# Gated recurrence on one core: score and value products cut into quarter-array products, units two deep

## The chip, the cores and the metric

The kernel runs on one core of a Trainium2 chip. The metric is the device time of one execution in microseconds. Engines are named as in the profile: PE (matrix products), DVE, ACT and POOL (vector, scalar and general engines), SP (the queue that issues most transfers). PE's weight loads are shown as PEld.

## The reference

Two blocks follow each other. The first is a gated linear recurrence over 4 batches, 8 heads, 768 tokens and head size 48; the second sends each of the 3072 tokens to the best of 8 experts.

```python
f = 1.0 / (1.0 + np.exp(-f_logit))
for t in range(S):
    state = f[:, :, t, :, None] * state + np.einsum('bhd,bhe->bhde', k[:, :, t], v[:, :, t])
    y[:, :, t] = np.einsum('bhd,bhde->bhe', q[:, :, t], state)
...
x = y.transpose(0, 2, 1, 3).reshape(3072, 384)
logits = x @ w_gate                       # 8 experts
expert_idx = np.argmax(logits, axis=1)
gate_w = softmax(logits)[arange, expert_idx]
h = np.maximum(x_sorted[lo:hi] @ w1[e], 0.0)      # 384 -> 1024, per expert
y_sorted[lo:hi] = h @ w2[e]                       # 1024 -> 384
out = gate_w[:, None] * y
```

## The kernel before, in words

The recurrence is done in 12 units. A unit is 128 tokens of two batches (16 heads, laid out as 8 slots with two heads of 64 partitions each, of which 48 are used). Units of even and odd number belong to the two pairs of batches, so a unit's state follows from the state two units earlier. All data are fp32, and every product on PE stands in the profile as two passes (a transposition as one).

For unit u these helpers exist; the lines are those of the profile:

- `load` (L410): f, k, q and v of the unit, on SP's queue. f has 2 buffers, k 3, q 4, v 3.
- `steps` (L420, L423, ACT): exp and ln of the gates. `total` (L430, DVE): their running sum, a scan of 1032 elements. `growth` (L444) and `decay` (L456), both ACT: exp of plus and minus that sum.
- `by_r` (L448, POOL): k times growth. `by_decay` (L468, DVE): q times decay. `ends` and `last_decay` (L451, L463): small copies on POOL.
- `score` (L473 to L483): k against q for half of the heads, eight products of 64 rows x 128 keys x 128 queries into two PSUM banks, and then DVE's `copy_predicated` under a causal mask into `at` (four such copies per unit, 512 elements each).
- `keys` and `keep` (L492 PE, L497 ACT): k transposed and copied to `kn`.
- `within` (L505): `at` with v into `yt`, 128 rows x 48 columns x 128 queries. `before` (L526): the old state with q, added to `yt`, 48 rows x 48 columns. `yt` is one buffer of two banks.
- `added` (L542) and `update` (L559 DVE, L561 POOL): the new state. `settle` (L567, ACT): the two copies of `yt` to `ys`.
- `rows` (L588 PE, L596 DVE): `ys` turned into rows of tokens (banks xp0 and xp1) together with the expert logits. `lay` (L613, L618, ACT) copies them to `xr`. Every second unit `choose` (L201 to L209, DVE), `weigh` (L241, ACT), `count` (L213, L214, PE into bank rp) and `settled` (`place` and `fill`, L220 to L247, DVE) find each token's expert and place, and `send` (L176) scatters the rows to `xs` on POOL's queue.

Three PSUM banks are handed round among kp0, kp1, xp0, xp1, dp and rp by `turns`; three more hold scores and two `yt`.

The order on every engine is written out by hand (`manual_schedule`): what a loop body calls first stands first on its engine. The loop of L687 runs n from 0 to 13, and its body works on unit n (scores, keys), unit n - 1 (`within`, `before`) and unit n - 2 (`settle`, `rows`, `lay`). On PE the order in the middle of the loop is: scores of the first half, kp, scores of the second half, xp, `within`, `before`, dp, and rp in every second step.

The last steps already start the experts: `soon` are the first rows of experts 0 and 1, loaded from `xs` when the scatters issued so far have landed; they are turned (etp), widened (L278) and narrowed (L292). After them 22 more expert tiles and two tiles of four parts each follow in an order of their own that the change does not touch. A fallback branch at the end is not taken.

Of the kernel before, what the change touches and what calls it, by code (L numbers as in the profile page):

```python
# [19 lines left out]
C = 128  # L20
NC = S // C
HP = H // 2
DP = 64

# [24 lines left out]
EARLY = 2  # L49
# [15 lines left out]
def _consts():  # L65
# [30 lines left out]
    m = {"causal": np.triu(np.ones((128, 128)))}  # L96
# [17 lines left out]
def kernel(  # L114
# [236 lines left out]
    with ExitStack() as st:  # L351
# [13 lines left out]
        scores = [wk.tile([128, 2, 2, HP, C], F32, name=f"at{i}", bufs=1) for i in range(2)]  # L365
        held = {
            n: [ld.tile([128, SEG, C], F32, name=f"{n}{i}") for i in range(bufs)]
            for n, bufs in (("q", 4), ("k", 3), ("f", 2))
# [10 lines left out]
        had, used = {"xp0": 0, "xp1": 1, "dp": 2, "rp": None}, [0, 1, 2]  # L379

        def turns(what, shape, steady=True):

            counts = had["rp"] is not None
            b = used[0]
            if steady:
                b = {
                    "kp0": had["dp"] if counts else had["xp0"],
                    "kp1": had["xp1"],
                    "xp0": had.get("kp0", 0),
                    "xp1": had["rp"] if counts else had.get("kp1", 1),  # L390
                    "dp": had.get("kp1", 1) if counts else had["dp"],
                    "rp": had["xp0"],
                }[what]
            had[what] = b
            if what == "dp":
                had["rp"] = None
            used.remove(b)
            used.append(b)
            return pst.tile(shape, F32, name=what, tag=f"tr{b}")

        def load(u, names, parts=(slice(None),)):
            x = units[u]
            for n in names:
                src = {"q": qu, "k": ku, "f": fu, "v": vu}[n]
                if n == "v":
                    x[n] = ld.tile([128, 2, H, D], F32, name=n, bufs=3)
                else:
                    x[n] = held[n][u % len(held[n])]
                for part in parts:
                    nc.sync.dma_start(x[n][:, part], src[u][:, part])  # L410
# [49 lines left out]
        def last_decay(u):  # L460
            x = units[u]
            x["last"] = wk.tile([128, SEG], F32, name="last", bufs=3)
            nc.gpsimd.tensor_copy(x["last"], x["dec"][:, :, C - 1])  # L463
# [9 lines left out]
        def score(u, a):  # L473
            x = units[u]
            x["at"] = scores[u % 2]
            ps = [pss.tile([128, HP, C], F32, name="s") for h in range(2)]
            for p, h, r in heads():
                s = HP * a + p
                nc.tensor.matmul(  # L479
                    ps[h][:, p], lhsT=x["k"][r, s], rhs=x["q"][r, s], start=True, stop=True  # L480
                )
            for h in range(2):
                nc.vector.copy_predicated(x["at"][:, a, h], _bc(causal, 1, HP), ps[h])  # L483

        def keys(u):
            x = units[u]
            x["kn"] = wk.tile([128, SEG, C], F32, name="kn", bufs=1)
            x["kp"] = []
            for a in range(2):
                kp = turns(f"kp{a}", [128, HP, C], u < NU - 2)  # L490
                for p in range(HP):
                    nc.tensor.transpose(kp[:, p], x["k"][:, HP * a + p], ident)  # L492
                x["kp"].append(kp)

        def keep(u):
            for a in range(2):
                nc.scalar.copy(units[u]["kn"][:, HP * a : HP * a + HP], units[u]["kp"][a])  # L497

        def within(u, a):

            x = units[u]
            if a == 0:
                x["yt"] = yt
            for p, h, _ in heads():
                nc.tensor.matmul(  # L505
                    x["yt"][DP * (h ^ a) : DP * (h ^ a) + D, a, p],
                    lhsT=x["v"][:, a, 2 * p + h],
                    rhs=x["at"][:, a, h, p],
                    start=p == 0,
                    stop=x["old"] is None,  # L510
# [3 lines left out]
        def before(u):  # L514

            x = units[u]
            if x["old"] is None:
                return


            for p in range(HP):
                for h in range(2):
                    for a in range(2):
                        r = slice(DP * h, DP * h + D)
                        to = DP * (h ^ a)
                        nc.tensor.matmul(  # L526
                            x["yt"][to : to + D, a, p],
                            lhsT=x["old"][r, HP * a + p],
                            rhs=x["q"][r, HP * a + p],
                            start=False,  # L530
                            stop=True,
                            skip_group_check=True,
                        )
# [17 lines left out]
        def update(u):  # L551

            x = units[u]
            new = wk.tile([128, SEG, D], F32, name="state", bufs=4)
# [8 lines left out]
        def settle(u):  # L563
            x = units[u]
            x["ys"] = wk.tile([128, 2, HP, C], F32, name="ys", bufs=1)
            for a in range(2):
                nc.scalar.copy(x["ys"][:, a], x["yt"][:, a])  # L567
# [3 lines left out]
        def rows(u):  # L571
# [12 lines left out]
            for a in range(2):  # L584
                j = 2 * (u - g[0]) + a
                xp = turns(f"xp{a}", [128, HP, XW], u < NU - 4)
# [9 lines left out]
                nc.vector.reduce_sum(  # L596
# [3 lines left out]
                )  # L600
# [27 lines left out]
        for i in (1, 0):  # L628
            nc.gpsimd.memset(scores[i], 0.0)
        warmth = pst.tile([128, C], F32, name="warmth", tag="tr2")  # L630

        def warm(count):

            for _ in range(count):
# [6 lines left out]
        load(2, "f")  # L641
        load(0, "v")
# [7 lines left out]
        for part in ab:  # L650
            steps(1, part)
        load(3, "f")
        load(2, "k")
        load(1, "v")
        load(2, "q")

# [10 lines left out]
        def settled(n, rt):  # L667
# [4 lines left out]
            if n == NU - 3:  # L672
# [7 lines left out]
            if n < NU:  # L680
# [5 lines left out]
        sends, later, decayed = [], None, None  # L686
        for n in range(NU + 2):  # L687
            here, back, last = n, n - 1, n - 2
            rt = None
            if here < NU:  # L690
                units[here]["old"] = states[here % 2]
            if 0 <= last:
                settle(last)
            if here < NU:
                score(here, 0)
            if 0 < n and n + 1 < NU:
                by_r(n + 1)
                ends(n + 1)
# [3 lines left out]
            if decayed:  # L702
                decayed()
                decayed = None
            if sends:
                now = sends if n >= NU - 1 else sends[:1]
# [3 lines left out]
            if n == 0:  # L710
                warm(2)
                keys(0)
                warm(4)
                for part in ab:
                    total(1, part)
                for part in ab:
                    growth(1, part)
                    by_r(1, part)
                    decay(1, part)
                    by_decay(1, part)  # L720
                    if part == ab[0]:
                        score(0, 1)
                warm(8)
                ends(1)
                last_decay(1)
                keep(0)
                steps(2)
                load(4, "f")
                load_consts()
                load_gate()  # L730
                load(3, "k")
                total(2)
                steps(3)
                growth(2)
            elif here < NU:
                if n == 1:
                    added(0)
                    decayed = update(0)
                keys(here)
                keep(here)  # L740
                score(here, 1)
            if 0 < n and n + 2 < NU:
                total(n + 2)
            if 0 <= last:
                rt = rows(last)
                if rt:
                    rt.choose()
            if 0 < n and n + 1 < NU:
                decay(n + 1)
                last_decay(n + 1)  # L750
            if 0 < n and n + 3 < NU:
                steps(n + 3)
            if 0 <= last:
                lay(last)
            if rt:
                rt.weigh()
            if 0 < n and n + 2 < NU:
                growth(n + 2)
            for a in range(2):
                if 0 <= back < NU:  # L760
                    within(back, a)
            if n == NU + 1:
                widen(soon[0], weights[0], early_h, range(3, 7))
            if n == NU:
                for x in soon:
                    turn_early(x)
            if 0 <= back < NU:
                before(back)
            if 0 < n and n + 1 < NU:
                for part in ab:  # L770
                    by_decay(n + 1, part)
            if n == 1:
                decayed()
            if 0 < here < NU and here // 2 < NC - 1:
                added(here)
                decayed = update(here)
            if rt:
                rt.count(turns("rp", [128, 2, rt.n, E], n < NU - 2))
                later = (n, rt)
                if n >= NU:  # L780
                    settled(*later)
                    later = None
# [381 lines left out]
```

## Time and profile before

| | us |
|---|---|
| median of 3 runs | 428.77 (427.64 to 429.92) |
| the profiled execution | 430.14 |
| its span, first to last instruction | 427.8 |
| PE busy in the span | 410.8 |
| DVE, ACT, POOL busy | 158.2, 105.3, 110.9 |
| n=2 and n=4 of the loop: first score starts | 28.23 and 47.46 |
| first product of the experts | 131.18 |
| first narrowing of an expert tile | 140.48 |

The profiled execution's time is 2.3 us above its span. In the tables of stretches each row is a stretch with its length, the busy time of PE, PEld, DVE, ACT and POOL with their instruction counts, the granted clock of PE (1.00 is full), the busy share of the DMA engines and their rate. In the timelines a row has start, length, engine, line, operation, written tile and read tiles, shape and count; a bracket tells how long the engine was idle before and what released it.

### The profile page before, as it was taken

What the parts mean: (1) busy time and instruction counts of PE and PEld (TensorE: products, weight loads), DVE (VectorE), ACT (ScalarE), POOL (GpSimd) and SP (SyncE); (2) the same over time, 40 slices, a digit from 0 to 9 for tenths busy, and PEclk for the clock granted to TensorE, in tenths of its full rate; (3) what the DMA queues carried; (4) which work ended last, traced back from release to release, by engine and by line L of the source; (5) the groups of instructions that cost most, each with busy time, mean ns of one, the idle gap of its engine ahead of it and who ended that gap; (6) DMA issues with size and microseconds to landing.
All of it is one profiled execution on the core that took longest, in us unless ns stands there. A gap on an engine that the chain in (4) does not pass through costs nothing.

```text
span 427.8 us, 8780 instructions
## 1 busy us (share of the span) xinstructions
PE 410.8 (96%) x3656; PEld 331.5 (78%) x3657; DVE 158.2 (37%) x365; ACT 105.3 (25%) x191; POOL 110.9 (26%) x121
## 2 busy tenths in 40 slices
PE   7979999999898999999999999999999999999992
PEld 7869888998788878888888888764888888888560
DVE  5887888888643521111111111211111111111110
ACT  6878766865332000000000000010000000000100
POOL 6484486779423200000000000000000000000000
PEclk9989999999998999999999999999999999999997
DMA  8969776869922369545695999810361399990000
GB/s 286 350 213 379 275 244 232 252 209 376 400 82 80 120 216 325 184 181 180 214 328 175 385 388 394 315 39 20 122 235 57 123 334 394 390 364 22 20 12 12
DMA packets 41982, 95.49 MB, mean 223 GB/s; under 512 B 3872, under 2 KB 27093, under 8 KB 41936
## 3 DMA queue, kind: packets, MB, share of 16 engines
q1 hardware_dynamic: 38448, 85.14, 56.2%
q0 software_dynamic: 3200, 9.64, 5.9%
q8 instruction: 30, 0.49, 0.5%
q10 hardware_dynamic: 288, 0.08, 0.1%
q14 instruction: 16, 0.13, 0.1%
HBM read 79.84 MB, written 15.40 MB: 223 GB/s over the span
## 4 chain that ended last, share of the span: by engine, by line
PE 91%; ACT 2%; DVE 2%; DMA 2%; POOL 1%; issue 1%; SPq 0%; POOLq 0%; ACTq 0%; DVEq 0%
PE hps L278 28%; PE yps L292 27%; PE xp L588 5%; PE s L479 5%; PE yt L505 5%; PE s L278 3%; PE yt L526 3%; PE kp L492 3%; PE yps L973 2%; PE hps L945 2%; PE yp L292 2%; PE etp L265 2%; PE dp L542 2%; DMA q<-in_qu_dram 2%; DVE sum L430 1%
## 5 line engine op out<-in xcount | busy, mean ns | idle before, releaser
L278 PEld LDWEIGHTS hps<-xT,w1t 128*128 128x128 f32 x1056 | 121.1, 192 | 7.3 <-issue 2.3
L278 PE MATMUL hps<-xT,w1t 128*128 128x128 f32 x1056 | 121.8, 275 | 0.0
L292 PE MATMUL yps<-w2t,hT 128*128 128x384 f32 x352 | 117.2, 486 | 0.0
L292 PEld LDWEIGHTS yps<-w2t,hT 128*128 128x128 f32 x352 | 65.2, 190 | 40.8
L176 POOL DMA_INDIRECT out_dram<-ysb,dst x26 | 25.3, 973 | 251.7 <-DVE ysb L299 251.7
L286 ACT ACTIVATE hT<-hps 128x512 f32<-128x512 f32 x22 | 13.2, 598 | 218.8 <-PE hps L278 218.8
L288 DVE TENSOR_SCALAR hT<-hps 128x512 f32<-128x512 f32 x22 | 15.2, 692 | 105.9 <-PE hps L278 105.9
L299 DVE TENSOR_SCALAR ysb<-yps,xrow 128x384 f32<-128x384 f32 x22 | 13.6, 618 | 92.9 <-PE yps L292 92.9
L176 POOL DMA_INDIRECT xs<-xr,posi x24 | 32.4, 1350 | 32.4 <-DVE lg L596 10.6
L483 DVE COPY_PREDICATED at<-mpack,s 128x512 f32<-128x512 uint8 x48 | 32.4, 728 | 14.3 <-PE s L479 10.9
L448 POOL TENSOR_TENSOR k<-k,r 128x1024 f32<-128x1024 f32 (+1 forms) x14 | 30.0, 2149 | 25.8 <-ACT r L444 25.7
L479 PE MATMUL s<-q,k 64*128 64x128 f32 x384 | 30.0, 290 | 5.3 <-DVE at L483 2.0
L479 PEld LDWEIGHTS s<-q,k 64*128 64x128 f32 x384 | 24.8, 191 | 9.0 <-DVE at L483 3.2
L430 DVE TENSOR_TENSOR_SCAN sum<-g,cap 128x1032 f32<-128x1032 f32 (+1 forms) x14 | 28.4, 2034 | 3.4 <-ACT g L423 3.4
L588 PE MATMUL xp<-fpack,ys 128*128 128x104 f32 x192 | 24.3, 280 | 0.8 <-ACT g L456 0.6
L588 PEld LDWEIGHTS xp<-fpack,ys 128*128 128x128 f32 x192 | 22.5, 192 | 2.2 <-issue 0.8
L505 PE MATMUL yt<-at,v 128*48 128x128 f32 x384 | 23.5, 275 | 0.0
L505 PEld LDWEIGHTS yt<-at,v 128*48 128x48 f32 x384 | 20.4, 123 | 1.2
L468 DVE TENSOR_TENSOR q<-q,g 128x512 f32<-128x512 f32 x24 | 17.6, 771 | 0.8 <-DMA q<-in_qu_dram 0.6
L267 DVE COPY xT<-etp 128x384 f32<-128x384 f32 x26 | 14.2, 548 | 3.2 <-remote 3.2
L567 ACT COPY ys<-yt 128x512 f32<-128x512 f32 x24 | 12.9, 593 | 9.7 <-PE yt L526 6.0
L497 ACT COPY kn<-kp 128x512 f32<-128x512 f32 x24 | 13.1, 602 | 5.5 <-PE kp L492 5.5
(113 smaller groups left out, 344.5 us busy)
## 6 DMA issues: line engine op xcount, KB each, us to landing
qw<-in_moe_w_dram SPq DMA_DIRECT2D x16, 1536.0 KB, 16.4
w1t<-in_moe_w_dram SPq DMA_DIRECT2D x8, 1536.0 KB, 6.8
w2t<-in_moe_w_dram SPq DMA_DIRECT2D x8, 1536.0 KB, 16.6
k<-in_ku_dram SPq DMA_DIRECT2D x12, 512.0 KB, 7.3
q<-in_qu_dram SPq DMA_DIRECT2D x12, 512.0 KB, 5.2
f<-in_fu_dram SPq DMA_DIRECT2D x11, 512.0 KB, 7.5
xrow<-xs SPq DMA_DIRECT2D x24, 200.0 KB, 7.5
xs<-pad SPq DMA_DIRECT2D x8, 600.0 KB, 3.5
```

What stands on the lines that cost most here:

```text
L176: ins = nc.gpsimd.indirect_dma_start(out=dst, out_offset=bass.IndirectOffsetOnAxis(ap=idx, axis=0), in_=src, in_offset=None, bounds_check= ...
L267: nc.vector.tensor_copy(x["xT"], tp)
L278: nc.tensor.matmul(hp[g][:, f, :], lhsT=w[0][:, j, b * 128 : b * 128 + 128], rhs=x["xT"][:, j, :], start=j == 0, stop=j == KD - 1,)
L288: nc.vector.tensor_scalar(x["hT"][:, 4:8], hp[1], 0.0, None, op0=OP.max)
L292: nc.tensor.matmul(yp, lhsT=x["hT"][:, f, :], rhs=w[1][:, f, :], start=f == 0, stop=f == NF - 1)
L430: nc.vector.tensor_tensor_scan(x["sum"][:, part].rearrange("p s c -> p (s c)"), x["g"][:, part].rearrange("p s c -> p (s c)"), cap[:, part ...
L448: nc.gpsimd.tensor_tensor(k, k, units[u]["r"][:, part], op=OP.mult)
L468: nc.vector.tensor_tensor(q, q, x["dec"][:, part], op=OP.mult)
L479: nc.tensor.matmul(ps[h][:, p], lhsT=x["k"][r, s], rhs=x["q"][r, s], start=True, stop=True)
L483: nc.vector.copy_predicated(x["at"][:, a, h], _bc(causal, 1, HP), ps[h])
L505: nc.tensor.matmul(x["yt"][DP * (h ^ a) : DP * (h ^ a) + D, a, p], lhsT=x["v"][:, a, 2 * p + h], rhs=x["at"][:, a, h, p], start=p == 0, st ...
L588: nc.tensor.matmul(xp[:, p], lhsT=x["ys"][:, a, p], rhs=wx[:, p, 0:XW] if a else wx[:, p, E:WX], start=True, stop=True,)
```

## The change

Scores and values are now products of a quarter of the array: 64 key rows by 64 (or 48) columns, on the four combinations of row group r and column group g. Keys are taken in halves. The first 64 keys meet all 128 queries ("long" products), the last 64 keys only the last 64 queries ("short" products); the masked quarter is not computed. So `at` has three parts in place of four, and three masks do the work of four. v gets a third copy in which halves are exchanged, so that keys and values stand on the same partitions.

`mix(n)` issues, in one run over the four quarters, the state products of unit n (`before`), the scores of unit n + 2 and the value products of unit n + 1 (`within`). Within that run `settle(n)` is called after the state products and the first mask after the scores of row group 0. A product of row group 0 into the third score bank is ordered behind the last mask (`behind`), because row group 1 writes the same bank earlier.

The banks are given out per step by `allot`. The loop has 10 steps; units 0 and 1 are started ahead of it, and the last two units are finished behind it by hand (`ordered_before`, `route`). k has 4 buffers, v 2, `state` 3, `last` 4. In the first loads v of unit 0, the constants and the gate weights now stand ahead of f of unit 2. In the profile of the new kernel the lines move: score L548 (long) and L558 (short), `within` L497 and L507, `before` L523, masks L606 and L611, dp L621, `update` L638, `settle` L646, xp L667 and L675, `lay` L693 and L698, kp L477 and L484, rp L215 and L216; the gates' lines L410 to L468 stay.

```diff
+    m = {"causal": np.arange(C)[None] >= p[:, None] % CH}
...
+        def allot(counts):
+            last = bank["dp"]
+            x, y = [b for b in used if b != last]
+            if counts:
+                bank.update(kp0=x, rp=y, kp1=last, xp0=x, xp1=last, dp=x)
+            else:
+                bank.update(kp0=x, kp1=y, xp0=last, xp1=x, dp=y)
...
-                    x[n] = ld.tile([128, 2, H, D], F32, name=n, bufs=3)
+                    x[n] = ld.tile([128, 3, H, D], F32, name=n, bufs=2)
...
+        def within(u, r, g):
+            x, on, i = units[u], slice(DP * r, DP * r + CH), g ^ r
...
+            def first(p):
+                nc.tensor.matmul(yt[DP * g : DP * g + D, r, p], lhsT=x["v"][on, 2 * r, 2 * p + i], rhs=x["at"][on, i, p], ...)
+            def second(p):
+                nc.tensor.matmul(yt[DP * g : DP * g + D, r, p, CH:C], lhsT=x["v"][on, 2 - r, 2 * p + i], rhs=late[on, HP * i + p], ...)
+            return [(2, first, p) for p in range(HP)] + [(1, second, p) for p in range(HP)]
...
+        def score(u, r, g):
...
+            def first(p):
+                nc.tensor.matmul(x["ps"][r][to, p], lhsT=x["k"][on, s, 0:CH], rhs=x["q"][on, s], ...)
+            def second(p):
+                ins = nc.tensor.matmul(late[to, HP * r + p], lhsT=x["k"][on, s, CH:C], rhs=x["q"][on, s, CH:C], ...).ins
+                if r == 0 and p == 0:
+                    behind(ins, x["masked"])
...
+        def mix(n):
+            score_banks(n + 2)
+            def parts(r, g):
+                long, short = score(n + 2, r, g)
+                inner = within(n + 1, r, g)
+                x = before(n, r, g)
+                if (r, g) == QUARTERS[-1]:
+                    x = x + [(0, settle, n)]
+                    inner = [(0, mask, n + 2, 0)] + inner
+                return x + short + long + inner if r else x + long + inner + short
+            run(parts)
...
         load(1, "kq")
+        load(0, "v")
+        load_consts()
+        load_gate()
...
-        load(2, "f")
-        load(0, "v")
+        load(2, "fk")
...
+        for n in range(NU - 2):
+            more = n < NU - 3
+            allot(bool(later))
+            by_decay(n + 3)
+            mix(n)
+            steps(n + 5)
+            mask(n + 2, 1)
+            mask(n + 2, 2)
+            load(n + 4, "q")
+            by_r(n + 3); ends(n + 3); last_decay(n + 3)
+            keys(n + 1, 0)
+            if later:
+                later[1].count(turns("rp", [128, 2, later[1].n, E]))
+            keys(n + 1, 1)
+            keep(n + 1)
+            if later:
+                settled(*later)
...
+            if sends: ...
+            total(n + 4)
+            rt = rows(n)
+            if rt:
+                rt.choose()
+                later = (n, rt)
+            lay(n)
+            if rt:
+                rt.weigh()
+            growth(n + 4); decay(n + 4)
+            added(n + 1)
+            update(n + 1)()
+            load(n + 5, "k"); load(n + 3, "v"); load(n + 7, "f")
+            if n in (5, 7):
+                load_weights((n - 5) // 2)
+        soon = [load_rows(slice(first[e], first[e] + C)) for e in range(EARLY)]
...
+        ordered_before(NU - 2, units[NU - 3]["summed"])
+        settle(NU - 2)
+        for x in soon:
+            turn_early(x)
+        later[1].count(...); settled(*later); ...
+        run(lambda r, g: within(NU - 1, r, g))
+        rt = route(NU - 2)
+        ordered_before(NU - 1, units[NU - 2]["summed"])
+        settle(NU - 1)
+        early_h = early_banks()
+        widen(soon[0], weights[0], early_h, range(3))
+        rt.count(...); settled(NU, rt)
+        rt = route(NU - 1)
+        widen(soon[0], weights[0], early_h, range(3, 7))
+        rt.count(...); settled(NU, rt)
+        widen(soon[0], weights[0], early_h, range(7, NF))
```

The loop's bounds on late units (`if n + 5 < NU` and the like) are left out here.

## The prediction

> **What bounds the kernel now.** I read the page's engine shares and slices first, then the busy time by stretch of two neighbouring steps, then the timeline of those steps on each engine.
>
> ```profile
> PE 410.8 (96%) x3656; PEld 331.5 (78%) x3657; DVE 158.2 (37%) x365; ACT 105.3 (25%) x191; POOL 110.9 (26%) x121
> PE   7979999999898999999999999999999999999992
> DVE  5887888888643521111111111211111111111110
> ...
> 66.30:75.45 9.15, 9.15 (x154) 8.21 (x153) 8.00 (x19) 5.73 (x12) 6.97 (x6) 1.00 0.70 259
> 75.45:85.15 9.70, 9.70 (x160) 8.72 (x157) 8.47 (x18) 8.33 (x16) 7.10 (x10) 1.00 0.80 243
> ```
>
> DVE's 37% is an average of two stages. In the recurrence (the first 13 slices, until the experts start near 131 us) it is 80 to 90% busy. In the two stretches (length, then busy us of PE, PEld, DVE, ACT and POOL, granted clock, DMA share) PE has no idle time and DVE only 1.2 us a step. After 140 us PE is full and the change does not reach it. So the forecast is the shift of that border.
>
> ```profile
> 75.45 1.16 PE L479 MATMUL s<-q,k 64*128 64x128 f32 x16
> 76.54 1.09 PE L492 MATMUL kp<-fpack,k 128*128 128x128 f32 x8
> 77.56 1.16 PE L479 MATMUL s<-q,k 64*128 64x128 f32 x16
> 78.65 2.03 PE L588 MATMUL xp<-fpack,ys 128*128 128x104 f32 x16
> 80.61 1.96 PE L505 MATMUL yt<-at,v 128*48 128x128 f32 x32
> 82.50 1.09 PE L526 MATMUL yt<-q,state 48*48 48x128 f32 x32
> 83.52 1.14 PE L542 MATMUL dp<-v,kn 128*64 128x48 f32 x32
> 84.59 0.41 PE L213 MATMUL rp<-oh,fpack 128*128 128x32 f32 x2
> ```
>
> Start to start this step is: scores 1.09 twice, kp 1.02, xp 1.96, yt 1.89 and 1.02, dp 1.07, and 0.56 for the rp pair in every second step.
>
> ```profile
> 68.75 0.74 DVE L220 COPY counts<-sums 128x8 f32<-128x8 f32 x1
> 70.88 0.18 DVE L247 RECIPROCAL xr<-su 128x4 f32<-128x4 f32 x1
> 72.19 2.30 DVE L430 TENSOR_TENSOR_SCAN sum<-g,cap 128x1032 f32<-128x1032 f32 x1
> 74.39 0.27 DVE L596 TENSOR_REDUCE lg<-xp 128x8 f32<-128x32 f32 x2
> 74.60 0.48 ACT L618 COPY xr<-xp 128x384 f32<-128x384 f32 x1 [2.35 <-DVE lg L596]
> 83.92 1.04 ACT L444 ACTIVATE r<-sum 128x1024 f32<-128x1024 f32 x1
> 84.86 1.06 ACT L567 COPY ys<-yt 128x512 f32<-128x512 f32 x2
> ```
>
> This is the chain to watch: L220 to L247 is `settled`, 2.31 us; the scan is 2.30; ACT's copy L618 starts 0.2 after the reduction; growth and the next copy stand 0.94 apart. Today xp ends at 71.5 and nobody on PE needs its banks for 3 us, because yt stands between xp and dp. The change moves yt away.
>
> **Products.** The records of L526 show four quarter products starting together every 109 ns, those of dp (64 columns of weights, 48 moving) two every 58 ns. A quarter now gets, per step, 12 long products (state, score, value) and 8 short ones (64 moving), each in two passes: 12 x 2 x 109 = 2.62 and 8 x 2 x 58 = 0.93, and 0.2 for the change of shape that every group shows: 3.75 us in place of 1.09 + 1.09 + 1.89 + 1.02 = 5.09. That is -1.34 a step. No row has short products on four quarters: if they go two at a time (29 ns each) the group is 4.7 us, if they run like the long ones in whole rounds 5.3, and 3.75 is the low end. I take 3.75, since four quarters at once are shown by L526 and 58 ns a round by dp; the rest goes into the range. The Trainium skill ("TensorEngine Tiling (Array Packing)", Instruction Overhead) speaks against short products: about 60 cycles each, 25 ns. By it the group is an estimated 4.2 us, and the sum some 5 us higher.
>
> DVE loses one mask of four, 0.68 us. v grows by half (192 KB a unit, 0.5 us at 370 GB/s); with 0.70 to 0.80 of DMA busy that stays hidden.
>
> **Where the gain goes.** The built program gives the waits. (a) The value products wait for both copies `settle`, which follow the state products of the same step. (b) In every second ("counting") step, the one with rp, dp shares its bank with xp0, so dp waits for ACT's L618 copy of xp0, which waits for DVE's reduction; on DVE, ahead of that reduction, stand the third mask, `settled` and the scan. (c) In the other ("choosing") step ACT's order is L618/L613, exp, growth, decay, and only then the next `settle`; exp waits for DVE's `choose` (1.2 us, six operations of 0.19). (d) The short scores of row group 0 wait for the first mask: it ends at 3.4 and 4.7 in the two steps below, PE arrives at 3.7 and 5.2, so this costs nothing until DVE is 0.3 later.
>
> Choosing step from its start 0: state products end at 1.07, settle 1.2 to 2.3, value products start at 2.4 (PE was ready at 1.96), the group ends 1.8 later at 4.2, kp and xp end at 7.15, dp at 8.2. DVE: third mask 4.3 to 5.0, scan to 7.3, reductions 7.6, choose 8.8. ACT: exp 9.0, growth and decay (0.96 each) 10.9.
>
> Counting step: ACT is free at 10.9 - 8.2 = 2.7, settle ends 3.75, value products start at 3.8: 1.85 us of PE lost. Group end 5.6, kp + rp + xp (3.54) 9.15. DVE: mask 5.7 to 6.35, settled to 8.7, scan 11.0, reduction 11.15, copy 11.65. dp starts 11.75, 2.6 us late, and ends at 12.8.
>
> Pair: 8.2 + 12.8 = 21.0 against 9.15 + 9.70 = 18.85. So PE's 2.7 us of a pair are returned, and 2.15 more. Behind dp on PE's queue stands the whole next group, so it is late next, and with it its masks; DVE itself would need only 16.4 (its operations of the pair with gaps 17.7, less two masks). POOL's product of k ends near 3.9 and is needed a step later. On SP the load of q goes at 1.1, lands after 5.2 to 7.5 and is needed 0.8 into the next step, so both are hidden, q with little to spare.
>
> **Sum.** Front: f of unit 2 is now issued behind v, the constants and the four gate loads, which wait for the constants. 4.3 MB lie ahead: 2.8 by 10 us, then 355 GB/s, so 14.4; gate loads 1.8 (their row), landing 3.5: 19.9 in place of some 17. k, v and f of unit 3 follow (1.6 MB, 24.4). ACT: steps of unit 3 to 26.6, growth and decay to 28.5; q times decay 1.3: the first new step starts at 30.1 (score of unit 2 now: 28.2). ACT then does unit 4's steps, growth and decay of unit 3 (after its scan, 32.2), settle to 35.3: the step ends at 41.3, the next at 50.3, where the old loop's n=4 starts at 47.46: +2.9. Three pairs: 63.0 for 56.6, +6.4. Step 8 (no scan, three small operations more): 11.0 for 8.7, +2.3. Tail, to the first `narrow_early` at 140.5: the old one takes 27.7 from 112.8 with broken PE work. Now step 9 takes 6.15; the last scatters leave POOL 14.1 after step 8's start, and as at present (113.46 to 119.2) rows can be fetched 5.7 later and land in 2.5; etp waits 4.3 us for that, then etp, rp, yt, xp, state, 8 blocks, xp and two rp: 19.9. 26.05 in all, -1.7. Together +9.9.
>
> **Clock.** PE's new idle times have a price of their own.
>
> ```profile
> 28.20:30.00 1.80, 1.77 (x19) 1.57 (x20) 1.51 (x3) 1.46 (x3) 1.80 (x2) 0.76 0.88 320
> 30.00:32.00 2.00, 2.00 (x13) 1.67 (x13) 0.84 (x2) 1.14 (x3) 2.00 (x3) 0.50 0.97 367
> ```
>
> The eighth column is the granted clock: 0.5 for 3.41 us, and kp there takes 1.97 for 1.02. It follows a 1.84 us gap; the 3.41 us stretch before it is 46% busy, another drop follows one of 61%, and stretches of 63 and 65% had none. Gaps of 1.85 and 2.6 us drop it about 0.8 and 1 times. A drop costs 1.7 us of work; I take half as hidden in the waits: 4 counting steps x 1.8 x 1.7 x 0.5 = 6.1, and 1.7 for the tail's gap: +7.8 (0 to 14). The Trainium skill ("TensorE: Matmul & The Clock Gate", HAM oscillation) has a half-rate clock only after gaps above about 3.4 us; by that alone nothing is lost in the steps, and the sum is +9.9 or a little more. The 1.84 us gap of this trace speaks against it.
>
> Total +17.7: the profiled execution takes 430.14 (span 427.8 and 2.3 around it) and would take 447.8; the median, 1.4 lower, becomes 446.5.
>
> **Rivals.**
> 1. Same stalls, clock stays up: +9.9, 438.7. For it: the drops need an unlucky place of the window. Chance 0.2.
> 2. Other side: the chain mask, settled, scan, reduction, copy does not reach dp. It decides once that chain takes under 3.6 us from the group's end in place of 6.1. Then DVE's 16.4 a pair bounds: 3 x -2.45, step 8 -1, tail -1.7, front +2.9: -7, 422. Against it: each member is a row above, and DVE runs in order. Chance 0.09.
> 3. Short products two at a time, or the half clock unhidden: 0.95 a step for ten steps, or 6 more: 453 to 456. Chance 0.13.
> 4. My case, 0.58.
>
> **Numbers.** 0.5%, 2.1 us, is about what a measurement can tell. Rival 2 holds 0.06 of faster and 0.03 of same; 0.02 of same comes from a cheaper front and tail: 0.06, 0.05, 0.89. The range runs from below rival 1 to rival 3's top: 435 to 457.
>
> **What would show it.** Right: dp (now L621) waiting over 2 us in every second step, released by L698; value products (L497) released by ACT's copy L646; choosing steps near 8 and counting steps near 13 us; 0.5 clock stretches between 50 and 130 us; etp late. Wrong: even steps of about 8.5 us, PE above 95% until 110 us, or the border before 131 us.

## The result, and the profile after

The changed kernel takes 455.62 us (454.23 to 456.75) where the kernel before takes 429.35: ratio 1.060, 95% interval 1.052 to 1.068. A second measurement gave 455.88 and 1.060 (1.052 to 1.068). The profiled execution took 456.75 with a span of 454.4; that is 26.6 longer than the span before.

The page's line of busy time and its rows of 40 slices (PE, DVE, granted clock):

```profile
PE 407.3 (90%) x4424; PEld 331.1 (73%) x4425; DVE 162.3 (36%) x343; ACT 104.1 (23%) x187; POOL 116.3 (26%) x121
PE   7767759695978799999999999999999999999992
DVE  6586776767573453111112111122111111221110
PEclk9968998989799989999999999999999999999998
```

PE is busy for 3.5 us less than before in a span that is 26.6 longer. The difference lies in the first 14 slices, before the experts: in most of them PE falls to 0.5 to 0.7, the clock dips in several, and DVE is busy for 4.1 us more in all, although it has one mask less in a unit. So PE waits, and the waits of PE say for what (line that waited, line that released it, us in total, times, longest):

```profile
PE yt L497 <- ACT ys L646: 13.0, 7, 3.9
PE s L558 <- DVE at L606: 9.6, 6, 5.0
PE dp L621 <- ACT xr L698: 7.0, 4, 2.2
PE xp L667 <- ACT ys L646: 2.3, 1, 2.3
```

The first is the wait for `settle`, (a) and (c) of the prediction, and the third is (b). The second, short scores behind the first mask, is (d), which I had at nothing. A counting step and the choosing step behind it, from PE's timeline:

```profile
60.99 0.27 PE L558 MATMUL s<-q,k 64*64 64x64 f32 x2 [0.76 <-DVE at L606]
61.60 0.66 PE L477 MATMUL kp<-fpack,k 128*128 128x128 f32 x4
62.94 2.03 PE L667 MATMUL xp<-fpack,ys 128*128 128x104 f32 x16
67.17 1.37 PE L621 MATMUL dp<-v,kn 128*64 128x48 f32 x32 [2.21 <-ACT xr L698]
68.48 1.96 PE L523 MATMUL yt<-q,state 48*48 48x128 f32 x32
```

xp ends at 65.0, dp starts at 67.17, and the state products behind it take 1.96 for 1.09: half clock. What stands behind the first of these waits is seen only when DVE and POOL are laid side by side:

```profile
57.72 2.59 DVE L468 TENSOR_TENSOR q<-q,g 128x1024 f32<-128x1024 f32 x1 [1.72 <-ACT g L456]
60.23 1.33 DVE L606 COPY_PREDICATED at<-mpack,s 128x512 f32<-128x512 uint8 x2
69.63 1.22 DVE L468 TENSOR_TENSOR q<-q,g 128x1024 f32<-128x1024 f32 x1
```

```profile
56.86 2.36 POOL L448 TENSOR_TENSOR k<-k,r 128x1024 f32<-128x1024 f32 x1
69.80 1.73 POOL L640 TENSOR_TENSOR state<-state,last 128x384 f32<-128x384 f32 x1 [0.73 <-DVE state L638]
```

DVE's product of q takes 1.22 us by itself. At 57.72 it meets POOL's product of k, which ends at 59.22, and it ends 1.1 us after that: it waited POOL out. Twelve us later DVE comes first, and POOL's small product takes 1.73 in place of 0.83. In the kernel before, the product of q stood at the end of a step, and POOL's product of k started after it had ended:

```profile
74.57 1.29 DVE L468 TENSOR_TENSOR q<-q,g 128x512 f32<-128x512 f32 x2
76.57 2.37 POOL L448 TENSOR_TENSOR k<-k,r 128x1024 f32<-128x1024 f32 x1 [0.44 <-ACT r L444]
```

In one table (us; a step starts with its state products, in the old loop with its first scores; steps 2, 4, 6, 8 of the new loop answer to n = 4, 6, 8, 10 of the old; "end" is the first `narrow_early`, the border behind which both kernels are alike):

| | step 2 starts | pair 2, 3 | pair 4, 5 | pair 6, 7 | step 8 | step 9 to end | end |
|---|---|---|---|---|---|---|---|
| before | 47.5 | 18.8 | 18.9 | 18.9 | 8.7 | 27.7 | 140.5 |
| predicted, clock left out | 50.3 | 21.0 | 21.0 | 21.0 | 11.0 | 26.05 | 150.4 |
| after | 54.95 | 23.4 | 22.3 | 25.3 | 12.3 | 28.2 | 166.35 |
| e1 dp's bank | 56.3 | 23.5 | 23.3 | 23.3 | 11.1 | 26.7 | 164.2 |
| e8 PE kept warm | 55.0 | 21.5 | 22.6 | 25.4 | 13.7 | 27.2 | 165.5 |
| e10 decay first | 53.8 | 21.4 | 22.0 | 23.9 | 12.9 | 26.3 | 160.4 |
| e9 all cures | 43.8 | 19.8 | 20.6 | 18.5 | 15.0 | 27.7 | 145.35 |
| e11 and late weights | 42.4 | 18.9 | 19.6 | 20.5 | 9.9 | 28.9 | 140.1 |

Steps 2 to 8 together take 65.3 us before, 74.0 as predicted without the clock, 83.2 after, 80.2 in e10, 73.8 in e9 and 68.8 in e11.

### The profile page after: what moved, and what is told of

It reads as the page before. It is cut to its first block, busy times and chain, and to the rows that moved or that the text cites. A ratio compares the mean times of both kernels' runs of the same rounds, so it can differ in the third digit from the quotient of the medians.

```text
span 454.4 us, 10248 instructions
## 1 busy us (share of the span) xinstructions
PE 407.3 (90%) x4424; PEld 331.1 (73%) x4425; DVE 162.3 (36%) x343; ACT 104.1 (23%) x187; POOL 116.3 (26%) x121
## 4 chain that ended last, share of the span: by engine, by line
PE 59%; DMA 1%; POOL 0%; DVE 0%; POOLq 0%; issue 0%
PE hps L280 26%; PE yps L294 25%; PE yps L1103 2%; PE hps L1075 2%; PE etp L267 2%; PE yp L294 1%; DMA out_dram<-ysb,dst 1%; DMA xrow<-xs 1%; PE hps L1094 0%; POOL out_dram L178 0%; DVE ysb L301 0%; POOLq L1142 0%
## 5 line engine op out<-in xcount | busy, mean ns | idle before, releaser
L290 DVE TENSOR_SCALAR hT<-hps 128x512 f32<-128x512 f32 x22 | 15.2, 692 | 106.2 <-PE hps L280 101.1
L178 POOL DMA_INDIRECT xs<-xr,posi x24 | 31.0, 1291 | 38.3 <-DVE xr L249 12.4
L468 DVE TENSOR_TENSOR q<-q,g 128x1024 f32<-128x1024 f32 (+1 forms) x14 | 29.1, 2087 | 13.7 <-ACT g L456 11.6
L448 POOL TENSOR_TENSOR k<-k,r 128x1024 f32<-128x1024 f32 (+1 forms) x14 | 29.7, 2126 | 16.6 <-ACT r L444 16.6
L497 PE MATMUL yt<-at,v 64*48 64x128 f32 x384 | 20.4, 292 | 13.3 <-ACT ys L646 13.0
L497 PEld LDWEIGHTS yt<-at,v 64*48 64x48 f32 x384 | 16.8, 132 | 14.9 <-ACT ys L646 14.7
L558 PE MATMUL s<-q,k 64*64 64x64 f32 x384 | 17.9, 239 | 10.2 <-DVE at L606 9.6
L667 PE MATMUL xp<-fpack,ys 128*128 128x104 f32 x192 | 25.0, 284 | 2.3 <-ACT ys L646 2.3
L548 PE MATMUL s<-q,k 64*64 64x128 f32 x384 | 24.8, 305 | 2.2 <-POOL rend L451 2.2
L667 PEld LDWEIGHTS xp<-fpack,ys 128*128 128x128 f32 x192 | 23.2, 196 | 3.1 <-ACT ys L646 2.4
L558 PEld LDWEIGHTS s<-q,k 64*64 64x64 f32 x384 | 15.9, 152 | 11.6 <-DVE at L606 10.7
L548 PEld LDWEIGHTS s<-q,k 64*64 64x64 f32 x384 | 20.3, 154 | 3.0 <-POOL rend L451 2.6
L621 PE MATMUL dp<-v,kn 128*64 128x48 f32 x320 | 12.6, 235 | 7.7 <-ACT xr L698 7.0
L621 PEld LDWEIGHTS dp<-v,kn 128*64 128x64 f32 x320 | 11.2, 148 | 9.1 <-ACT xr L698 7.6
```

Source lines behind the costliest of these rows:

```text
L178: ins = nc.gpsimd.indirect_dma_start(out=dst, out_offset=bass.IndirectOffsetOnAxis(ap=idx, axis=0), in_=src, in_offset=None, bounds_check= ...
L290: nc.vector.tensor_scalar(x["hT"][:, 4:8], hp[1], 0.0, None, op0=OP.max)
L448: nc.gpsimd.tensor_tensor(k, k, units[u]["r"][:, part], op=OP.mult)
L468: nc.vector.tensor_tensor(q, q, x["dec"][:, part], op=OP.mult)
L497: nc.tensor.matmul(yt[DP * g : DP * g + D, r, p], lhsT=x["v"][on, 2 * r, 2 * p + i], rhs=x["at"][on, i, p], start=p == 0, stop=False, skip ...
L548: nc.tensor.matmul(x["ps"][r][to, p], lhsT=x["k"][on, s, 0:CH], rhs=x["q"][on, s], start=True, stop=True,)
```

## Experiments

Theory A: the units two deep tie PE, ACT and DVE into a ring (decay, product of q, masks, `settled`, scan, reduction, ACT's copies, decay of the next step), and each named wait is only the place where PE feels it. Rivals: one wait alone is the price; or the half clock is; or the engines have no slack in any order. Four kernels ran on a chip where the kernel before takes 423.9 us, the others where it takes 428.6 to 430.2, so ratios are compared, and steps in the profile.

**after_again: the changed kernel once more.**

> The changed kernel itself, unedited, beside the three that follow, because the kernel before takes 429.4 us on one chip and 423.9 us on another. Expected: ratio 1.052 to 1.068 as at first, first narrow_early near 166 us in the profile.

455.88 us against 430.15; first `narrow_early` at 166.8. This is the yardstick.

**e1: dp in another bank.**

```diff
-                bank.update(kp0=x, rp=y, kp1=last, xp0=x, xp1=last, dp=x)
+                bank.update(kp0=x, rp=y, kp1=last, xp0=x, xp1=last, dp=y)
```

> In counting steps dp takes rp's bank instead of the bank of xp0. Theory A (DVE's chain mask, settled, scan, reduction sets the pace and the bank is only where PE feels it): the four dp waits for ACT's L698 (2.2, 2.2, 2.2, 0.35, together 7.0 us) go, but L698 stays as late as before, so exp, growth, decay and the settle of the choosing step behind it on ACT are as late, and the value products L497 of the choosing step, which waited 0 in step 3, wait some 2 us: 453 to 457 us. Theory B (the shared bank alone is the price): dp starts 2.2 us earlier, nothing takes the place of the wait, and two or three half-clock stretches of 3.41 us go with it: 444 to 449 us.

453.32 us, ratio 1.069 (1.067 to 1.071). The waits of PE from 20 to 140 us:

```profile
PE yt L497 <- ACT ys L646: 20.5, 10, 4.0
PE s L558 <- DVE at L606: 11.5, 9, 2.8
PE s L548 <- POOL rend L451: 0.4, 1, 0.4
```

```profile
PEclk9686999999899899999999999999999999999998
```

This is theory A: dp's 7.0 us are gone from the list, the value products wait 20.5 where the changed kernel's wait 12.7 in this stretch, and a pair is still 23.3 to 23.5. The granted clock is full here from 44 to 118 us, which speaks against the clock too.

**e2: `settled` and the sends behind `rows`.**

```diff
-            if later:
-                settled(*later)
...
             rt = rows(n)
+            if later:
+                settled(*later)
...
```

> settled and the sends are issued behind rows, so DVE reduces xp right after the scan and L698 copies xp0 some 2 us earlier; dp keeps its bank. Theory A (DVE's chain is the cause): dp's waits of 2.2 us fall below 0.5 us, ACT is early too, a counting step is 2.2 us shorter, three or four of them, and one or two half-clock stretches go: 444 to 450 us. Theory B (only the bank): the same for dp. Rival: settled now stands between the reductions and choose or the state update of dp, and the scatters leave later; the tail gives back 1 to 3 us: 450 to 455 us.

455.18 us, ratio 1.074 (1.068 to 1.081). dp waits 1.0 us in all for L698, but the short scores 13.9 and the value products 15.2. The expected 444 to 450 did not come: I had let DVE's 2.3 us of `settled` vanish, where by DVE's order they only move behind the reduction and ahead of the next product of q.

**e3 and e10: decay before growth.** The same kernel, on the chip of each group.

```diff
-                growth(n + 4)
                 decay(n + 4)
+                growth(n + 4)
```

(and alike for units 2 and 3 ahead of the loop, with `by_decay(2)` ahead of growth).

> ACT computes decay before growth, so DVE's product of q can start before POOL's product of k. Theory A (the product of q, 2.5 to 3.1 us beside POOL's product of k and 1.22 us alone, waits for POOL to finish, and this makes the first mask late): L468 falls to 1.2 to 1.5 us in the loop, the waits of the short scores L558 inside the loop (0.75 to 1.2 us in each step that has one) go, the first step starts some 1.3 us earlier: 447 to 452 us. Rival (the product of q is slow for another reason, such as the loads, or the first mask waits for the scores anyway): L468 stays at 2.5 us or more, or L558 waits as before: 454 to 457 us.

445.64 us, ratio 1.0527 (1.0485 to 1.0569).

> The exchange of growth and decay alone, once more, on the chip of these runs, because the kernel before took 423.9 us on the chip where it was run and 430 us where the changed kernel was. Theory A (DVE's product of q waits for POOL's product of k): 9 to 13 us under the changed kernel's 455.7, ratio 1.03 to 1.04 if the kernel before takes 430 us here. Rival (most of the 12 us seen in the profile were the chip's or the clock's luck): within 5 us of the changed kernel, ratio 1.048 or more.

452.44 us (449.84 to 456.74), ratio 1.0554 (1.0485 to 1.0623). DVE and POOL of this second run, at the same place as above:

```profile
55.66 1.23 DVE L468 TENSOR_TENSOR q<-q,g 128x1024 f32<-128x1024 f32 x1 [0.78 <-ACT g L456]
56.65 2.46 POOL L448 TENSOR_TENSOR k<-k,r 128x1024 f32<-128x1024 f32 x1 [0.85 <-ACT r L444]
```

The mechanism is shown: DVE comes first and needs 1.23, and POOL's product of k grows by 0.1 for an overlap of 0.24 us. In the three meetings shown in rows, and in two more of this run (77.32 and 78.31 us), the one that starts later grows by the overlap less 0.12 to 0.15. The mean of the ten whole products of q falls from 2.42 to 1.53. The waits of PE from 20 to 140 us, three of the lines:

```profile
PE yt L497 <- ACT ys L646: 12.8, 8, 4.0
PE dp L621 <- ACT xr L698: 7.0, 4, 2.3
PE s L558 <- DVE at L606: 5.9, 2, 4.6
```

Inside the loop one wait of the short scores is left, 1.3 us in step 7, where the product of q waited for the load of q and so came behind POOL again. The size is not what theory A asks for: 3.4 us by the median (5.3 if the longest of the four runs, 456.74, is left out), with intervals that overlap the changed kernel's, and 6 and 12 us at the border of the two profiles. The ratio of 1.055 is where the rival has it: most of the 12 us of e3's profile does not come back. dp still waits 7.0 and the value products 12.8 us: the rest of the ring stands.

**e4: growth and decay behind `settle`.**

```diff
             mix(n)
+            growth(n + 3); decay(n + 3)
...
             mask(n + 2, 2)
+            by_decay(n + 3)
...
-            growth(n + 4); decay(n + 4)
```

> growth and decay of unit n+3 are issued on ACT behind the settle of step n, and DVE's product of q behind the three masks. Theory A (the value products wait because settle stands behind growth and decay on ACT): the waits of L497 for L646 fall from 13.0 us in seven to under 4 us, first mask no longer late, L558 waits gone; dp still waits about 2 us in counting steps, where DVE's chain grows by the product of q: 440 to 450 us. Rival (DVE becomes the bound, as its product of q now waits for POOL's product of k at the place that the scan needs): steps of 11 us or more, 453 to 460 us.

446.37 us, ratio 1.055 (1.051 to 1.058), above the expected 440 to 450 once the faster chip is allowed for. L497's waits fall from 12.7 to 5.1 and the short scores' inside the loop to 0.3, but dp waits 8.3, and there is a new wait: xp for ACT's copies of kp (L484), 5.8 us, because growth and decay now stand ahead of them, besides `steps`.

**e5 and e8: products of a constant in PE's waits.** e5 puts 13 and 16 of them into each counting step, e8 6 and 8 (steps 0 and 1 have 24 and 13, and 15 and 6).

```diff
+        def busy(b, count):
+            warmth = pst.tile([128, C], F32, name="warmth", tag=f"tr{b}")
+            for _ in range(count):
+                nc.tensor.matmul(warmth, lhsT=pad[:, 0:C], rhs=pad[:, 0:C], start=True, stop=True)
...
+                    inner = [(0, busy, bank["kp0"], count)] + inner     # ahead of the value products
...
+                if counting:
+                    busy(bank["rp"], 8)
                 added(n + 1)
```

> Products of a constant are put on PE into its waits: 13 ahead of the value products of every counting step (24 and 13 in the first two steps) and 16 ahead of dp in counting steps, each some 0.11 us at full clock, so about as long as the waits of 1.75 and 2.2 us. Nothing else moves. Theory A (the clock that the waits cost has a price of its own, 6 us in the steps): half-clock stretches fall from eight windows of 3.41 us to five or fewer, waits for DVE and ACT keep their ends, and the time is 3 to 7 us under the changed kernel. Rival (the half clock falls into time that PE would wait anyway): fewer stretches, but within 1.5 us of the changed kernel, or later by the dummies that overrun a wait.

457.45 us, ratio 1.064 (1.057 to 1.072), no half clock from 30 us on. But one such product took 0.24 us, not 0.11, so they were 1.4 to 1.6 us longer than the waits of 1.75 and 2.2 us, and this run settles nothing.

> The products of a constant again, in a number that fits the waits: one took 0.24 us, so 6 (1.5 us) ahead of the value products of a counting step, 8 (1.9 us) ahead of its dp, 15 and 6 in the first two steps. Theory A (the half clock has a price of its own; the run with twice as many paid it back by overrunning each wait by 1.4 us): choosing steps at 8.1 us in place of 9.4 to 9.8, counting steps at 12 to 13, a pair 20.5 to 21.5 us in place of 23.4, first narrow_early at 158 to 163 us, 4 to 8 us under the changed kernel. Rival (the ring of waits sets the pair and the clock is hidden in it): a pair stays at 23 us, within 1.5 us of the changed kernel.

454.45 us, ratio 1.056 (1.054 to 1.059). Its waits from 20 to 140 us (lines stand 6 later here: L612, L627, L652 and L704 are L606, L621, L646 and L698) and its clock by slices:

```profile
PE s L558 <- DVE at L612: 9.2, 7, 3.8
PE yt L497 <- ACT ys L652: 2.5, 6, 1.0
PE dp L627 <- ACT xr L704: 1.2, 3, 0.4
```

```profile
PEclk9869999999999989999999999999999999999998
```

From 33 to 158 us there is no half clock, where the changed kernel has 17 us of it between 37 and 120. Choosing steps 3 and 5 take 8.2 and 8.3 in place of 9.8 and 9.4, the length predicted for full clock. But up to the start of step 8 the choosing steps gain 2.2 us in all and the counting steps lose 0.8, step 8 takes 1.4 more, and the border comes 0.9 us earlier; by the medians it is 1.4 us, with intervals that overlap. By the time the rival is right. The price of the clock itself is bounded, not measured: in step 6 these products end 1.2 us behind the `settle` that the value products wait for (in step 4 too, but there a wait for the first mask follows), in step 8 1.4 us behind the copy that dp waits for. With these added back, an estimate of 0.9 to 3.5 us is left. Most of the half clock in the loop lies in time that PE has to wait anyway.

**e6: ACT's order, dp's bank and both together.** Decay ahead of growth behind `settle`, `steps` behind `keep`, dp in bank y:

```diff
             mix(n)
+            decay(n + 3); growth(n + 3)
-            steps(n + 5)
...
             keep(n + 1)
+            steps(n + 5)
```

> All three waits of the loop at once: ACT's order is settle, decay and growth of unit n+3, the copies of kp, then the steps of unit n+5; DVE's product of q stands behind the masks; dp takes rp's bank in counting steps. Theory A (each single cure only moved the wait to the next member of a ring of ACT, DVE and PE; with all of them PE is the bound again): dp's and the short scores' waits gone, value products at most 0.7 us late, a pair of steps 18.5 to 20 us in place of 23.4, first narrow_early at 142 to 150 us: ratio 1.00 to 1.035. Rival (DVE's and ACT's own work, some 8.2 us a step plus the product of q waiting for POOL, bounds the loop now): a pair stays at 21 us or more and new waits for DVE or ACT appear: ratio 1.045 or more.

448.02 us, ratio 1.042 (1.035 to 1.049): between the two, in its pairs (20.1 to 23.1) as well. The value products still wait 15.9 us from 20 to 140. `settle` stands right behind ACT's copies of xp, these are behind DVE's reduction, and that is behind the product of q, which meets POOL's again (2.7 us), and the scan.

**e7: the same, and the constants behind unit 2's loads.**

```diff
         load(0, "v")
-        load_consts()
-        load_gate()
...
         load(2, "q")
+        load_consts()
+        load_gate()
```

> The same as the run before it, and the constants and gate loads are issued behind f, k and q of unit 2, so SP does not wait for the constants ahead of f of unit 2. Theory A (the front is set by f of unit 2, which is issued at 16.6 us): f of unit 2 is issued near 6 us, the first step starts 4 to 7 us earlier, and the whole shift reaches the end: 4 to 7 us under the run before it. Rival (what is loaded later, f of unit 3, q of unit 2 or the constants, becomes late instead, or the DMA engines are full until 13 us anyway): at most 2 us.

444.88 us, ratio 1.035 (1.027 to 1.044). f of unit 2 is issued at 6.1 us in place of 16.6, and step 2 starts 2.5 us earlier than in e6. f of unit 4 is now the one behind the gate loads: it is issued at 24.9 in place of 21.9. The gain of 3.1 us lies between the two expectations.

**e9: all cures.** To e7 are added: the gate loads behind v of unit 2, `settle(0)` ahead of the loop, decay first for unit 2, and in the loop

```diff
             mix(n)
+            if later:
+                later[1].weigh()
...
             mask(n + 2, 1)
+            by_decay(n + 3)
             mask(n + 2, 2)
-            by_decay(n + 3)
...
-            total(n + 4)
             rt = rows(n)
             if rt:
                 rt.choose()
+            total(n + 4)
             lay(n)
-            if rt:
-                rt.weigh()
```

> All cures together: ACT settle, decay, growth, copies of kp, steps; the first settle already in the prologue; dp in rp's bank; DVE takes the product of q between the second and third mask, before POOL's product of k can start, and the scan behind choose; the exp of choose goes behind the next settle; f of unit 2 ahead of the constants, and the gate loads behind f of unit 4. Theory A (the products themselves are 0.9 us a step cheaper and only the ring of waits and the front ate it): steps of 8.7 to 9.5 us, first step near 25 us, first narrow_early at 132 to 141 us, ratio 0.98 to 1.01. Rival (DVE, ACT and PE each have about 8.5 us of work a step, and any order leaves some wait): steps of 10 us or more, ratio 1.02 to 1.035.

433.70 us, ratio 1.007 (1.004 to 1.010). Its largest waits of PE from 20 to 140 us, six of its lines:

```profile
PE s L558 <- issue: 4.7, 4, 2.7
PE yt L497 <- ACT ys L646: 2.5, 8, 0.4
PE xp L667 <- ACT ys L646: 2.2, 1, 2.2
PE rp L215 <- issue: 1.9, 1, 1.9
PE yt L523 <- issue: 1.2, 2, 0.9
PE yt L497 <- issue: 0.9, 3, 0.4
```

22 of the 26 us are back. The three waits of the loop are down from 29.3 us (L497, L558 and L621 in the changed kernel, 20 to 140 us) to 3.5. Of the 21.0 us by which the border comes earlier, 11.1 lie ahead of step 2, where no run cured the loads alone, and 9.4 in steps 2 to 8. The ratio is where theory A has it, but the steps, 8.9 to 11.3 us and 15.0, are longer than its 8.7 to 9.5: the ring accounts for about half of the loss, and for the steps the rival is not refuted. Step 2 starts 3.6 us ahead of the kernel before; the steps behind it still take 8.5 us longer than that kernel's, 6.3 of this in step 8. What is left has no partner engine: PE stands for 9 us, 6.8 of it at its quarter products, and the rows name no cause.

**e11: weights of the second expert later.**

```diff
-            if n in (5, 7):
-                load_weights((n - 5) // 2)
+            if n == 5:
+                load_weights(0)
         soon = [load_rows(...) for e in range(EARLY)]
+        load_weights(1)
```

> The kernel with all cures, and the weights of the second expert are loaded behind the rows of the first tiles instead of in step 7, where DMA is full. In the run with all cures PE stands for 9 us in the loop and tail at its quarter products without a wait that the profile names (issue), the longest 2.68 us in step 8 while the DMA engines are full with these weights, followed by 3.4 us of half clock. Theory C (PE's own instructions are fetched over the full DMA engines): the 2.68 us and the half clock behind it go, issue waits fall to 5 to 6.5 us: 4 to 5 us less, 428 to 430.5 us, ratio 0.995 to 1.002. Rival (the stalls have another cause, such as a wait that the profile does not record): issue waits stay at 8 us or more and the time within 1.5 us of 433.7; or the later weights make the second expert wait: above 435.

431.23 us, ratio 1.0046 (1.0007 to 1.0085), against e9's 1.0073 (1.0044 to 1.0102). Step 8 falls from 15.0 to 9.9 and the stall of 2.68 us in it is gone, as theory C has it. But others came (L497 1.9, xp 1.3, rp 1.1 us), so 7.3 us of them are left, more than theory C allowed and less than its rival. The time does not decide it.

The traces say more, since they also hold the packets that carry instructions (16 KB each, about 1 us long). The longest stall and its packet:

```profile
111.17 0.21 PE L558 MATMUL s<-q,k 64*64 64x64 f32 x1 [2.68 <-issue]
q8 instruction: 1, 0.02, 1.2%
```

The second row is the only such packet from 107 to 112 us. It runs from 108.8 to 109.8 us, and PE goes on 1.4 us after its end. The same holds for all seven stalls of 0.8 us and more in e9 and e11: each ends 1.2 to 1.5 us behind the end of an instruction packet, and in the two us ahead of that packet and during it DMA was at 0.88 to 1.06. From 20 to 140 us these two traces have 38 such packets, 13 of them with DMA under 0.7; none of the 13 is followed by a stall in this way. So theory C is well supported: PE waits for instructions that come late while DMA is full. It is not proved, since no run moved the packets alone, and a packet under full DMA does not always bring a stall: the kernel before has no stall behind its packets with DMA at 1.0. No kernel here beats the one before, and in steps 2 to 8 none is as fast; e9 and e11 come near it by their earlier front.

## Why the prediction was right, and where it was not

Slower was right, and 455.6 lies inside 435 to 457, 9 us above the 446.5. By the profile's stages the front is 4.7 us above its sum (54.95 for 50.3), steps 2 to 8 are 3.1 above theirs (83.2 for 74.0 and 6.1 of clock) and the tail is 0.5 above (28.2 for 26.05 and 1.7 of clock). The products and the wait (d) were priced too low and the clock too high, and these partly cancel: that the steps came out so near is in part luck.

**Products: mis-sized.** Rounds are as predicted: 109 ns for long products, 55 to 58 ns for short ones, four at once. But the group takes 4.15 us net of waits (step 2 of e11: 46.80 - 42.36 less a wait of 0.29), not 3.75. The gain is 0.9 us a step, not 1.34. The excess is in the changes from one kind of product to the next, where I took 0.2. The 4.2 set beside it is nearer, but not by a price per product, since the rounds are no longer than I took them. The bound of 5.3 for short products in whole long rounds is a wrong sum: 20 x 2 x 109 ns and 0.2 give 4.6.

**Waits (a), (b), (c): right.** dp waited 2.2 us (2.6 predicted), released by L698, in each of the three pairs; value products waited 1.75, 0.9, 1.6 and 2.6 us in counting steps (1.85 predicted). e1, e2 and e4 show that the waits are one ring: the prediction added them up along one pair, and did not say that curing one lengthens another.

**Wait (d): the step that failed.** "This costs nothing until DVE is 0.3 later", and in the front "q times decay 1.3". Both took the product of q at its duration in the old trace, where it never met POOL's product of k. The change puts it right behind decay, and POOL's product right behind growth. In eight of ten units it takes 2.5 to 3.1 us, the first mask is late, and the short scores wait 0.75 to 1.2 us in five steps of the loop; with DVE first, in e10, all but one of these go, and the one left stands behind a late load of q. The prediction had that load hidden "with little to spare"; in the changed kernel too the product of q of step 7 waits 1.4 us for it. The 5.0 us in the front are another place of the same wait: there the first mask of unit 1 stands on DVE behind the scan of unit 2, which waits for f, and with f early, in e7, 0.5 is left.

The Trainium skill ("SBUF — State Buffer", Summary: rules for kernel authors) says this of DVE and GpSimd: when a DVE operation has two SBUF inputs and the GpSimd one reads SBUF, the second to issue fully blocks until the first is done. The rows above agree, in both orders (2.59 for 1.22, 1.73 for 0.83). I had not weighed it.

**Clock: right in kind, wrong in price.** Half clock came: 27 us of it from 20 to 170 us by the granted clock, where before had 7. In steps 2 to 8 it is 13.7 us, four stretches of 3.4, one each at dp's waits of 2.2 us in steps 2 and 4 and two in a row at that of step 6, where the sum has 7.2 drops. The Trainium skill ("TensorE: Matmul & The Clock Gate", HAM oscillation) warns of gaps above some 3.4 us; in the steps from 2 on the longest gap is 2.6, and half clock came all the same. But +6.1 for the steps was too much: e1's three pairs at full clock are together only 0.8 us shorter, and e8 leaves an estimated 0.9 to 3.5 us. More than the half that I took was hidden, since a ring that waits does not care how fast PE reaches the wait.

**Front: undersized.** Step 2 starts at 54.95, +7.5 in place of +2.9. 1.3 of it is the blocked product of q of unit 2; the first `settle` behind `steps`, growth and decay cost PE 3.9 us in step 0 and 2.0 in step 1, and half clock from 37.2 to 40.6 lies in step 0. That f of unit 2 is issued at 16.6 us behind the gate loads was seen and priced.

**Steps and tail.** Pairs of 23.4, 22.3 and 25.3 against 21.0 + 1.5 of clock; step 8 12.3 for 11.0. The tail took 28.2 for 26.05: etp waited 0.9 us, not 4.3, but step 9 took 8.2 us, not 6.15, and xp waited 2.3 us for the last `settle` (L646). Nine of the thirteen profiles of the new code have this wait of xp, 1.7 to 2.3 us; e1 to e4 have longer waits of etp instead (2.4 to 5.2). No run explains it.

**Rivals.** Rival 2, that DVE's chain does not reach dp, was wrong as built; e9 and e11 are close to the kernel that it described (dp waits 0.3 to 0.7 us), and yet they reach 1.005, not 0.98, since the products gain less and PE meets stalls that no engine releases.

## What to carry to other kernels

When work moves between steps, take the duration of each moved DVE or POOL operation again: what counts is which operation of the other engine it now stands beside, not what it took in the old place. When several waits lie on one ring of engines, curing one moves its time to the next, and pricing them one by one, half clock included, counts the same time twice: price the longest way round the ring, and test a cure by the length of the pair, not by whether its wait is gone. A group of products that is cheaper on PE helps only as far as ACT and DVE, here busy for 30 and 36 of the 40 us from 55 to 95 in e11, have slack to follow.

## What the runs showed of the hardware that was not expected

- DVE's fp32 product of two SBUF operands and POOL's wait for each other whole: 2.59 us beside POOL, 1.22 to 1.23 ahead of it; it is the one that starts later that pays, the overlap less some 0.13 us.
- 17 us of half clock in the loop cost an estimated 0.9 to 3.5 us, because for most of it PE would have waited anyway.
- PE stands for 9.0 us in e9 and 7.3 in e11 (20 to 140 us) with no wait that the rows name, 1.1 in the changed kernel and 1.4 in the one before. DMA is busier in e9 and e11 (0.81 to 0.95 from 55 to 95 us, against 0.62 to 0.65 in the changed kernel and 0.71 to 0.74 in the one before), and the longest stall, 2.68 us, fell into three us with DMA at 1.0. Instructions come over DMA too, 0.59 MB in 36 packets of 16 KB on this queue of the changed kernel (packets, MB, share):

```profile
q8 instruction: 36, 0.59, 0.5%
```

The Trainium skill ("Runtime: NRT & Kernel Launch", Instruction fetch mechanics) has such blocks fetched ahead and the cost of crossing into the next mostly hidden. These traces differ from that where DMA is full: the stalls of 0.8 us and more all end 1.2 to 1.5 us behind the end of an instruction packet. e11 removed one of them and not the others, and no run here proves the cause.
